# Attention with key tiles in twos: two score tiles, then P-V of the two before

## The chip, the cores and the metric

The kernel runs on one core of a Trainium2 chip. The time is the device time in microseconds (us) from launch to end. Five engines work beside one another, each through its own queue in order: TensorE (PE, matmul), VectorE (DVE), ScalarE (ACT), GpSimd (POOL) and SyncE (SP), which here issues nearly all transfers. TensorE writes its results to eight PSUM banks of 128 partitions by 512 fp32 numbers. VectorE and ScalarE read them there; GpSimd doesn't.

## The reference

Two layers of multi-query attention, each followed by a SwiGLU feed-forward, on 2048 tokens of width 448, all in fp32:

```
def A(x):  # 16 heads of 28, one shared key and value head
    q, k, v = x @ wq (per head), x @ wk, x @ wv
    p = softmax(q k^T * 28**-0.5)
    return (p v, heads side by side) @ wo
def B(x):  # width 1792
    return (silu(x @ w_gate) * (x @ w_up)) @ w_down
x = x + A(layernorm(x)); x = x + B(layernorm(x))
x = x + A(layernorm(x)); x = x + B(layernorm(x))
```

## The kernel before, in words

**Stages.** Projections of q, k and v, then the attention proper (`scores`), then the feed-forward, twice. The change is in `scores` alone. There is a second pass of the whole forward that runs only where row sums leave a bound (`full`); it isn't run here.

**Groups and steps.** Attention runs over 16 groups (`GR`: four chunks of 512 queries by four groups of four heads). In each group it goes over the 16 key tiles of 128 keys; one key tile is a step. A step issues, on TensorE, the transposed scores of four heads (lines 564 to 570): three waves of four matmuls, where the four heads sit on four strips of 32 rows of the array and the three waves are the parts of a product of split fp32 numbers. Three heads go to a tile of three banks (`three`, of which there are two, taken in turn) and the fourth to a single bank, bank 7 (`one`). ScalarE turns the single (line 573) and then the three (line 574) into exponentials in SBUF (`pt1`, `pt`). No maximum is subtracted there; it is folded into the scores by extra rows of q and k.

**P-V.** `pv` (line 604) multiplies the exponentials by the values (`vsb`, with a column of ones that gives the row sums). Its four heads sit on four strips of 32 columns of the array, and it is fp32, which shows as two matmul rows for each of the four. It runs two steps behind the scores and adds up in bank 6 over all 16 tiles of a group.

**End of a group.** `post` copies bank 6 to SBUF on VectorE (line 617) and gathers the four row sums with four transfers (line 620). `rest`, two steps later (`due`), waits for them, tests and inverts them on VectorE (lines 626 to 628), sends them to DRAM and back as a broadcast (630, 631), and on GpSimd normalises (638) and splits the result in high and low halves (lines 134, 135).

**What else is issued in a group.** The order of every queue is that of the program text. By key tile: `stack`, the q loads of the group after next, at tile 4 (line 380); `parts`, their split on GpSimd, at 7; `rows`, the transfer that puts the maxima into the split q and therefore waits for the split, at 9 (line 391); `load_wo` in groups 2 and 3 and `weights` (feed-forward weights, five transfers and a split on GpSimd) in groups 11 to 13, both at 8. In groups 5, 13 and 14 the steps of a layer norm come one per tile from tile 6: four statistics (`stat`, VectorE), `scale` (GpSimd: the reciprocal deviation `rstd`, lines 221 and 222) and, in 5 and 13, four `apply` (VectorE, line 229, which reads `rstd`). In groups 4, 8 and 12, at tile 10, `between_steps` puts the output projection of a chunk on TensorE, 48 matmuls into the free three and into bank 7, with four sums on VectorE; in 8 and 12 two flips (transposes) with it.

Of the kernel before, what the change touches and what calls it, by code (L numbers as in the profile page):

```python
# [8 lines left out]
F32 = mybir.dt.float32  # L9
F32R = mybir.dt.float32r  # L10
AF = mybir.ActivationFunctionType
ALU = mybir.AluOpType
# [3 lines left out]
P = 128  # L16
# [6 lines left out]
NT = S // P  # L23
# [3 lines left out]
FG = 2  # L27
SCALE = DH ** -0.5
# [26 lines left out]
def forward(  # L55
# [14 lines left out]
    nc = tc.nc  # L70
    fine, least, whole = fine or (None, None, None)
    KC = NC
# [14 lines left out]
    phase, banks, threes, live, turn = ExitStack(), [], [], set(), {}  # L87
# [33 lines left out]
    def halves(name):  # L121

        return pers.tile([P, 2, 512], F32R, tag="halves", name=name, bufs=2)
# [18 lines left out]
    vsb = pers.tile([P, NT, 32], F32, name="vsb")  # L142
# [158 lines left out]
    GR = [(c, g) for c in range(NC) for g in range(NG)]  # L301

    class Attention:
# [226 lines left out]
        def scores(self, ff):  # L530
            next(switch)
            with tc.tile_pool(name=f"at{self.layer}", bufs=1) as wp:
                woh = wp.tile([P, NG, D], F32R, name="woh")
                wol = wp.tile([P, NG, D], F32R, name="wol")
                on, accs, pts = {}, {}, {}
                todo, due = [], {}
# [21 lines left out]

                def step(n):

                    i, kt = divmod(n, NT)
                    three, one = threes[n % 2], banks[7]
                    q, k, ks = qts[i % 3], keys[kt // 4], slice(P * (kt % 4), P * (kt % 4) + P)
                    for z, (kp, part) in enumerate(((0, 0), (1, 0), (0, 1))):
                        for j in range(4):
                            js = slice(32 * j, 32 * j + 32)
                            nc.tensor.matmul(  # L567
                                three[:, j, :] if j < 3 else one, k[js, kp, ks], q[js, part, :],
                                start=(z == 0), stop=(z == 2), tile_position=(32 * j, 0),
                            )  # L570
                    pt = wp.tile([P, 3, 512], F32, name="pt", bufs=3)
                    pt1 = wp.tile([P, 512], F32, name="pt1", bufs=2 if full else 3)
                    nc.scalar.activation(pt1, one, AF.Exp, scale=SCALE)  # L573
                    nc.scalar.activation(pt, three, AF.Exp, scale=SCALE)  # L574
                    pts[n] = [*(pt[:, j, :] for j in range(3)), pt1]

                def between_steps(n):

                    i, kt = divmod(n, NT)
                    free, one = threes[(n + 1) % 2], banks[7]  # L580
                    if full:
                        self.lent = free[:, 0, :]
                        self.advance(KC)
                        if kt == 11 and i + 1 < len(GR):
                            self.places[i + 1](free[:, 1, :])
                    if not todo or kt != 10:
                        return
                    c = todo.pop()
                    ks = list({8: (0, 1), 12: (2, 3)}.get(i, ()))
                    adds = []  # L590
                    for t in (1, 2, 3):
                        adds.append(outproj(c, t, free[:, t - 1, :]))
                        if ks:
                            flip(got, X0, [ks.pop(0)], one)
                    for f in adds:
                        f()
                    outproj(c, 0, one)()

                def pv(n):
                    i, kt = divmod(n, NT)  # L600
                    if kt == 0:
                        accs[i] = banks[6]
                    for j in range(4):
                        nc.tensor.matmul(  # L604
                            accs[i][32 * j : 32 * j + 32, :], vsb[:, kt, :], pts[n][j],
                            start=(kt == 0), stop=(kt == NT - 1), skip_group_check=True,
                        )
                    del pts[n]
                    if kt == NT - 1:
                        due[n + 4] = post(i)  # L610

                def post(i):

                    c, g = GR[i]
                    out2 = halves("o2").bitcast(F32)
                    oraw, rb = out2[:, 0, :], out2[:, 1, :]
                    nc.vector.tensor_copy(oraw, accs.pop(i))
# [32 lines left out]
                last = NT * len(GR)  # L650
                for n in range(last):
                    i, kt = divmod(n, NT)
                    if kt == 4 and 2 < i + 2 < len(GR):
                        self.stack(i + 2)
                    if kt == 7 and 2 < i + 2 < len(GR):
                        self.parts(i + 2)
                    if kt == 9 and 2 < i + 2 < len(GR) and not full:
                        self.rows(i + 2)
                    if i in (2, 3) and kt == 8:
                        load_wo(i - 2)  # L660
                    if n == NT and ff.nxt:
                        ff.nxt.below(nc.sync)
                    if kt == 8 and 10 < i <= 11 + FG:
                        ff.W[i - 11] = weights(i - 11)
                    step(n)
                    if not full:
                        between_steps(n)
                    if n > 1:
                        pv(n - 2)
                    if full:  # L670
                        between_steps(n)
                    if n in due:
                        due.pop(n)()
                    if i in (5, 13, 14) and kt > 5:
                        for f in {5: fs, 13: fs1, 14: ff.second[0][:5]}[i][kt - 6 : kt - 5]:
                            f()
                for n in (last - 2, last - 1):
                    pv(n)
                self.lent = None
                next(switch)  # L680
                ff.X[0] = X0
# [223 lines left out]
    fs, got = norm_steps(0)  # L905
# [64 lines left out]
```

## Time and profile before

| | us |
|---|---|
| three runs: median (lowest to highest) | 2043.53 (2042.91 to 2044.38) |
| profiled execution, span from first to last instruction | 2041.5 |
| attention of the first layer, first to last exponential's start | 73.9 to 593.0 |
| attention of the second layer | 1082.9 to 1601.4 |
| busy: TensorE / ScalarE / VectorE / GpSimd | 2018.5 / 1311.0 / 460.0 / 536.7 |

The page gives the profiled execution by its span; the runs' median is 2.0 us above it. In a row of a group stand the line, the engine, the operation, output from input with their shapes, the count, the busy time in us, the mean in ns of one and the idle time ahead of it with what ended it. In a row of the timeline stand the start, the duration, the engine, the line and the operation; a bracket gives the idle time ahead of it. Rows of the same kind that lie close are merged (x4). In a row of a table of stretches stand the stretch, its length, the busy time and count of each engine (PE, weight loads, DVE, ACT, POOL), the granted clock of TensorE (0.99 to 1.00 in both attention stages), the share of the DMA engines and GB/s.

### The profile page before, as it was taken

The page shows a single profiled execution, that of the slowest core. Times are in us where ns is not written, and L with a number is a line of the kernel's source. Part 1 is how long each engine was busy: PE and PEld are TensorE (multiplying, and loading weights), DVE is VectorE, ACT ScalarE, POOL GpSimd, SP SyncE. Part 2 cuts the span into 40 slices and gives each one's busy share as a digit, 9 for nine tenths or more (in the row PEclk, how much of TensorE's full clock was granted, in tenths as well). Part 3 has the DMA queues.
Part 4 walks back from the last instruction along what each step waited for, and adds up shares of the span by engine and source line. Part 5 has one row for each costly group of instructions (what it writes and reads, how often), then busy time and mean ns, then how long its engine had stood idle before and what let it go on. Part 6 is the DMA issues. An engine that isn't in the chain of part 4 may idle for free.

```text
span 2041.5 us, 43675 instructions
## 1 busy us (share of the span) xinstructions
PE 2018.5 (99%) x18627; PEld 1275.7 (62%) x18627; DVE 460.0 (23%) x890; ACT 1311.0 (64%) x2152; POOL 536.7 (26%) x601
## 2 busy tenths in 40 slices
PE   8999999999999999999999999999999999999998
PEld 7533434334348999999883334343343689988887
DVE  6300101001104323222451001010011242232322
ACT  3699898997973333333348998979979533333332
POOL 4313121021302333333341221111222122333320
PEclk9999999999999999999999999999999999999999
DMA  4201000011100111100031110100110000111102
GB/s 146 66 22 28 21 12 22 12 37 27 32 12 19 31 31 31 31 16 26 21 93 34 30 30 12 22 12 22 27 45 13 25 17 20 31 31 31 31 1 74
DMA packets 76512, 63.44 MB, mean 31 GB/s; under 512 B 22904, under 2 KB 63224, under 8 KB 76312
## 3 DMA queue, kind: packets, MB, share of 16 engines
q1 hardware_dynamic: 74580, 58.93, 10.4%
q8 instruction: 147, 2.41, 0.5%
q10 hardware_dynamic: 1732, 1.66, 0.3%
q14 instruction: 53, 0.43, 0.1%
HBM read 47.72 MB, written 12.32 MB: 29 GB/s over the span
## 4 chain that ended last, share of the span: by engine, by line
PE 50%; ACT 46%; DVE 1%; issue 1%; DMA 1%; POOL 0%; ACTq 0%; SPq 0%; DVEq 0%; POOLq 0%
PE bank L292 39%; ACT pt L574 31%; ACT pt L573 15%; PE bank L272 4%; PE three L551 2%; PE bank L551 2%; PE bank L246 1%; PE bank L604 1%; DMA wr<-in_A_wk_dram 1%; PE three L567 0%; DVE xl L253 0%; DMA kt<-stage 0%; DVE xn L229 0%; PE bank L398 0%; DVE vt L505 0%
## 5 line engine op out<-in xcount | busy, mean ns | idle before, releaser
L574 ACT ACTIVATE pt<-three 128x1536 f32<-128x1536 f32 x512 | 741.2, 1448 | 0.0
L604 PE MATMUL bank<-pt,vsb 128*32 128x512 f32 x4096 | 547.0, 606 | 0.5 <-ACT pt L574 0.5
L567 PEld LDWEIGHTS three<-qstack,keys 32*128 32x128 f32 x4608 | 252.9, 183 | 449.7 <-ACT pt L573 393.2
L567 PE MATMUL three<-qstack,keys 32*128 32x512 f32 x4608 | 498.5, 426 | 2.3 <-DVE vt L505 1.1
L567 PE MATMUL bank<-qstack,keys 32*128 32x512 f32 x1536 | 493.5, 426 | 2.9 <-ACT pt L573 2.9
L292 PE MATMUL bank<-xh,wgh 64*128 64x512 f32 x1728 | 447.6, 390 | 0.4
L292 PE MATMUL bank<-xh,wgl 64*128 64x512 f32 x1404 | 368.2, 390 | 0.0
L573 ACT ACTIVATE pt<-bank 128x512 f32<-128x512 f32 x512 | 305.8, 597 | 74.3 <-PE bank L567 68.1
L292 PE MATMUL bank<-xl,wgh 64*128 64x512 f32 x1296 | 335.1, 390 | 0.0
L292 PE MATMUL bank<-wdh,h 64*128 64x448 f32 x1792 | 331.2, 364 | 1.2 <-ACT h L827 0.8
L292 PEld LDWEIGHTS bank<-xh,wgh 64*128 64x128 f32 x1728 | 262.9, 184 | 19.1 <-DVE xl L253 1.5
L743 POOL TENSOR_TENSOR xres<-stage,xres 128x448 f32<-128x448 f32 x108 | 127.4, 1199 | 497.9 <-ACT stage L742 497.9
L638 POOL TENSOR_TENSOR o<-o 128x512 f32<-128x512 f32 x32 | 41.1, 1285 | 821.5 <-DMA o<-rd 748.5
L292 PEld LDWEIGHTS bank<-wdh,h 64*128 64x128 f32 x1792 | 242.5, 184 | 15.2 <-issue 2.7
L567 PEld LDWEIGHTS bank<-qstack,keys 32*128 32x128 f32 x1536 | 244.3, 183 | 4.5 <-ACT pt L573 4.3
L299 ACT COPY seen<-bank 128x1 f32<-128x1 f32 x664 | 81.7, 163 | 247.3 <-PE bank L292 244.4
L292 PEld LDWEIGHTS bank<-xh,wgl 64*128 64x128 f32 x1404 | 216.6, 184 | 13.8
L292 PE MATMUL bank<-wdl,h 64*128 64x448 f32 x896 | 217.7, 366 | 0.0
L825 ACT ACTIVATE sg<-bank 128x512 f32<-128x512 f32 x112 | 67.3, 601 | 220.0 <-PE bank L292 214.9
L292 PEld LDWEIGHTS bank<-xl,wgh 64*128 64x128 f32 x1296 | 196.3, 184 | 10.5
L604 PEld LDWEIGHTS bank<-pt,vsb 128*32 128x32 f32 x4096 | 80.9, 108 | 190.0 <-issue 175.2
L826 DVE TENSOR_TENSOR sg<-bank,sg 128x512 f32<-128x512 f32 x112 | 77.4, 691 | 500.0 <-ACT sg L825 491.1
(115 smaller groups left out, 1736.6 us busy)
## 6 DMA issues: line engine op xcount, KB each, us to landing
o<-rd SPq DMA_DIRECT2D x32, 256.0 KB
qd<-stage SPq DMA_DIRECT2D x32, 224.0 KB
qraw<-qd SPq DMA_DIRECT2D x128, 56.0 KB
wdr<-in_B_w_down_dram SPq DMA_DIRECT2D x28, 224.0 KB
wr<-in_B_w_gate_dram SPq DMA_DIRECT2D x28, 192.0 KB
wr<-in_B_w_up_dram SPq DMA_DIRECT2D x28, 192.0 KB
out_dram<-xres SPq DMA_DIRECT2D x15, 224.0 KB
wrk<-kt SPq DMA_DIRECT2D x8, 256.0 KB
```

The costliest lines, as they stand in the source:

```text
L272: nc.tensor.matmul(po, a, b, start=(i == 0), stop=(i == len(seq) - 1))
L292: nc.tensor.matmul(po, a, b, start=start, stop=stop, skip_group_check=True)
L299: nc.scalar.copy(seen[:, i : i + 1], po[:, 0:1])
L551: nc.tensor.matmul(po[:, 0:D], a[:, g, ts_], b[:, g, :], start=(g + z == 0), stop=(g == NG - 1 and z == 2))
L567: nc.tensor.matmul(three[:, j, :] if j < 3 else one, k[js, kp, ks], q[js, part, :], start=(z == 0), stop=(z == 2), tile_position=(32 * j, 0),)
L573: nc.scalar.activation(pt1, one, AF.Exp, scale=SCALE)
L574: nc.scalar.activation(pt, three, AF.Exp, scale=SCALE)
L604: nc.tensor.matmul(accs[i][32 * j : 32 * j + 32, :], vsb[:, kt, :], pts[n][j], start=(kt == 0), stop=(kt == NT - 1), skip_group_check=True,)
L638: nc.gpsimd.tensor_tensor(rb, oraw, rb, ALU.mult)
L743: nc.gpsimd.tensor_tensor(r, s, r, ALU.add)
L825: nc.scalar.activation(sg, pg[0], AF.Silu)
L826: nc.vector.tensor_tensor(sg, pg[1], sg, ALU.mult)
```

## The change

The 16 key tiles of a group go in eight cycles of two. In cycle m the two banks 6 and 7 are single a and single b, and they change roles from cycle to cycle. A cycle issues:

1. TensorE: scores of the even tile into the first three and single a; ScalarE: exponential of a, then of the three.
2. TensorE: scores of the odd tile into the second three and single b; VectorE copies b to SBUF (`pt1`); ScalarE: exponential of the three, then of the copy, in place.
3. The norm steps of this cycle, if any (now two per cycle, from cycle 3).
4. TensorE: P-V of both tiles of the cycle before, into single a; VectorE copies the result to SBUF (first cycle of a group) or adds it to what is there.
5. `rest` of a finished group (in cycle 2 of the next one), and the output projection (cycle 5), which uses the first three and single b.

So the sum over a group's tiles is in PSUM over two tiles and in SBUF over the eight cycles; `post` has no copy of its own. `pt` and `pt1` have four buffers in place of three. `stack` stands at cycle 2, `parts` at 3, and at 4 `rows`, `load_wo` and `weights`, in this order.

```diff
-                def step(n):
+                def tile_scores(n, three, one):
...
-                    three, one = threes[n % 2], banks[7]
...
-                    pt = wp.tile([P, 3, 512], F32, name="pt", bufs=3)
-                    pt1 = wp.tile([P, 512], F32, name="pt1", bufs=2 if full else 3)
-                    nc.scalar.activation(pt1, one, AF.Exp, scale=SCALE)
-                    nc.scalar.activation(pt, three, AF.Exp, scale=SCALE)
+                    pt = wp.tile([P, 3, 512], F32, name="pt", bufs=4)
+                    pt1 = wp.tile([P, 512], F32, name="pt1", bufs=4)
                     pts[n] = [*(pt[:, j, :] for j in range(3)), pt1]
+                    return pt, pt1
+
+                def singles(m):
+                    return banks[6 + m % 2], banks[7 - m % 2]
+
+                def cycle(m):
+                    a, b = singles(m)
+                    pt, pt1 = tile_scores(2 * m, threes[0], a)
+                    nc.scalar.activation(pt1, a, AF.Exp, scale=SCALE)
+                    nc.scalar.activation(pt, threes[0], AF.Exp, scale=SCALE)
+                    pt, pt1 = tile_scores(2 * m + 1, threes[1], b)
+                    nc.vector.tensor_copy(pt1, b)
+                    nc.scalar.activation(pt, threes[1], AF.Exp, scale=SCALE)
+                    nc.scalar.activation(pt1, pt1, AF.Exp, scale=SCALE)
...
-                def pv(n):
-                    i, kt = divmod(n, NT)
-                    if kt == 0:
-                        accs[i] = banks[6]
-                    for j in range(4):
-                        nc.tensor.matmul(
-                            accs[i][32 * j : 32 * j + 32, :], vsb[:, kt, :], pts[n][j],
-                            start=(kt == 0), stop=(kt == NT - 1), skip_group_check=True,
-                        )
-                    del pts[n]
-                    if kt == NT - 1:
-                        due[n + 4] = post(i)
+                def pv(m, to):
+                    i, u = divmod(m, NT // 2)
+                    for y in range(2):
+                        n = 2 * m + y
+                        for j in range(4):
+                            nc.tensor.matmul(
+                                to[32 * j : 32 * j + 32, :], vsb[:, n % NT, :], pts[n][j],
+                                start=(y == 0), stop=(y == 1), skip_group_check=True,
+                            )
+                        del pts[n]
+                    if u == 0:
+                        accs[i] = halves("o2").bitcast(F32)
+                        nc.vector.tensor_copy(accs[i][:, 0, :], to)
+                    else:
+                        nc.vector.tensor_tensor(accs[i][:, 0, :], to, accs[i][:, 0, :], ALU.add)
+                    if u == NT // 2 - 1:
+                        due[m + 3] = post(i)
...
+                ops = {}
+                for i, todo_ in ((5, fs), (13, fs1), (14, ff.second[0][:5])):
+                    for n, f in enumerate(todo_):
+                        ops.setdefault((i, 3 + n // 2), []).append(f)
...
+                    cycle(m)
+                    for f in ops.get((i, u), ()):
+                        f()
+                    if m:
+                        pv(m - 1, singles(m)[0])
+                    if m in due:
+                        due.pop(m)()
+                    between_cycles(m)
+                pv(last - 1, banks[6])
```

More of the change, by code (lines that the diff above doesn't have):

```diff
@@ L649, in scores @@
                 ff.second = norm_steps(2)
[L650 to L653, printed above, removed]
+                ops = {}
+                for i, todo_ in ((5, fs), (13, fs1), (14, ff.second[0][:5])):
+                    for n, f in enumerate(todo_):
+                        ops.setdefault((i, 3 + n // 2), []).append(f)
+                last = NT // 2 * len(GR)
+                for m in range(last):
+                    i, u = divmod(m, NT // 2)
+                    if u == 2 and 2 < i + 2 < len(GR):
                         self.stack(i + 2)
-                    if kt == 7 and 2 < i + 2 < len(GR):
+                    if u == 3 and 2 < i + 2 < len(GR):
                         self.parts(i + 2)
-                    if kt == 9 and 2 < i + 2 < len(GR) and not full:
+                    if u == 4 and 2 < i + 2 < len(GR) and not full:
                         self.rows(i + 2)
-                    if i in (2, 3) and kt == 8:
+                    if i in (2, 3) and u == 4:
                         load_wo(i - 2)
-                    if n == NT and ff.nxt:
+                    if m == NT // 2 and ff.nxt:
                         ff.nxt.below(nc.sync)
-                    if kt == 8 and 10 < i <= 11 + FG:
+                    if u == 4 and 10 < i <= 11 + FG:
                         ff.W[i - 11] = weights(i - 11)
[L665 to L678, printed above, removed]
+                    cycle(m)
[7 more added lines that the diff above has]
+                pv(last - 1, banks[6])
                 self.lent = None
```

21 lines of the change are left out of this document (10 added, 11 removed).

## The prediction

> **What bounds the kernel now.** First the page: totals and the costly groups.
>
> ```profile
> span 2041.5 us, 43675 instructions
> ...
> PE 2018.5 (99%) x18627; PEld 1275.7 (62%) x18627; DVE 460.0 (23%) x890; ACT 1311.0 (64%) x2152; POOL 536.7 (26%) x601
> ...
> L573 ACT ACTIVATE pt<-bank 128x512 f32<-128x512 f32 x512 | 305.8, 597 | 74.3 <-PE bank L567 68.1
> ```
>
> TensorE is busy almost throughout, so the question is what paces the attention stages. I looked at their length and at ScalarE's waits in them.
>
> ```profile
> 73.90:593.00 519.10, 517.61 (x5245) 196.84 (x5249) 49.10 (x144) 484.34 (x511) 105.04 (x106) 0.99 0.09 22
> ```
>
> ```profile
> ACT pt L573 <- PE bank L567: 68.1, 10, 11.3
> ```
>
> The first layer's 256 steps run 519 us from the first exponential to the last. The second layer has the same stage, so I put half of the 68.1 us of long waits into each; 255 intervals in 519.1 - 34.1 = 485.0 us are 1.90 us per key tile, 3.80 per pair. The waits are the out-projections (11.3 us the longest). In between, ScalarE shows no idle time and looks like the bound. The timeline behind one out-projection says otherwise.
>
> ```profile
> 494.46 0.60 ACT L573 ACTIVATE pt<-bank 128x512 f32<-128x512 f32 x1 [11.33 <-PE bank L567]
> 494.95 1.45 ACT L574 ACTIVATE pt<-three 128x1536 f32<-128x1536 f32 x1
> 496.28 0.60 ACT L573 ACTIVATE pt<-bank 128x512 f32<-128x512 f32 x1
> ...
> 498.09 0.63 ACT L573 ACTIVATE pt<-bank 128x512 f32<-128x512 f32 x1
> ...
> 501.89 0.60 ACT L573 ACTIVATE pt<-bank 128x512 f32<-128x512 f32 x1
> ...
> 503.77 0.60 ACT L573 ACTIVATE pt<-bank 128x512 f32<-128x512 f32 x1
> ```
>
> ```profile
> 493.08 0.50 PE L567 MATMUL three<-qstack,keys 32*128 32x512 f32 x3
> ...
> 493.42 0.40 PE L567 MATMUL three<-qstack,keys 32*128 32x512 f32 x3
> ...
> 493.65 0.40 PE L567 MATMUL three<-qstack,keys 32*128 32x512 f32 x3
> ...
> 493.99 1.06 PE L604 MATMUL bank<-pt,vsb 128*32 128x512 f32 x8
> 494.98 0.51 PE L567 MATMUL three<-qstack,keys 32*128 32x512 f32 x3
> 495.11 0.49 PE L567 MATMUL bank<-qstack,keys 32*128 32x512 f32 x1
> ...
> 501.37 0.39 PE L567 MATMUL bank<-qstack,keys 32*128 32x512 f32 x1
> ```
>
> Where scores stood ready, ScalarE made two steps in 498.09 - 494.46 = 3.63 us, 1.815 each. Later it needs 503.77 - 501.89 = 1.88. TensorE, by contrast, goes from scores to scores in 494.98 - 493.08 = 1.90 although ScalarE stood idle before: it isn't waiting, it is that slow. One step has 0.91 for scores (493.08 to 493.99) and 0.99 for P-V. So TensorE paces the steps, and ScalarE has 0.08 us of hidden slack per step: its rows overlap (0.60 long, but the next starts 0.49 later), so the slack is no gap on the page.
>
> Why 0.91: the second and third waves of four matmuls are 0.23 apart, but the last wave holds the array 0.34 (493.65 to 493.99) before P-V starts. Each change between scores and P-V costs about 0.1.
>
> **The change part by part: the pace.** Two score tiles in a row, then two P-V tiles in a row, so two changes per pair go. The end of the layer has two P-V together already:
>
> ```profile
> 592.79 1.92 PE L604 MATMUL bank<-pt,vsb 128*32 128x512 f32 x16
> 594.99 1.06 PE L604 MATMUL bank<-pt,vsb 128*32 128x512 f32 x8 [0.27 <-ACT pt L574]
> ```
>
> Sixteen matmuls span 1.92 where eight span 1.06, and the next work starts 0.07 before a span's end (493.99 + 1.06 against 494.98), so a P-V pair holds TensorE 1.85 against 1.98. A score pair is 0.34 + 4 x 0.23 + 0.34 = 1.60 against 1.82. TensorE alone could do a pair in 3.45. That isn't the new pace, since three other chains close each cycle. Time 0 is the start of the first single's exponential:
> - ScalarE: 2 x 1.815 = 3.63, and one of the four now reads SBUF. The nearest rows are a 512-wide cast from SBUF and the single's exponential from PSUM: 621 - 597 = 24 ns, so 3.65.
> - Single a: exponential 0.60, release 0.05 (494.46 + 0.60 to the single's matmul at 495.11), P-V pair 1.85, scores to their third wave 0.57, wave to exponential 0.52 (501.37 to 501.89): 3.59.
> - VectorE: P-V pair ends at its span's 1.92, VectorE starts 0.14 later (594.99 + 1.06 to 596.19), sum 0.69, release 0.05, rest of the scores and drain 0.8: 3.60.
>
> ```profile
> L827 ACT CAST h<-sg 128x512 fp32r<-128x512 f32 x112 | 69.6, 621 | 99.3 <-DVE sg L826 87.2 <-POOL onl L135 12.1
> ```
>
> ```profile
> L617 DVE COPY o<-bank 128x512 f32<-128x512 f32 x32 | 22.1, 692 | 659.1 <-PE bank L604 659.1
> ```
>
> ```profile
> 596.19 0.69 DVE L617 COPY o<-bank 128x512 f32<-128x512 f32 x1 [22.47 <-PE bank L604]
> ```
>
> All three lie within 0.1 of each other, so I take the largest, 3.65 (bounds: 3.59, if ScalarE overlaps better than it has shown, and 3.80, if VectorE's 512 new operations arrive late). Gain (3.80 - 3.65) x 256 pairs = 38.4 us; bounds 54 and 0. The copies and sums themselves, 512 x 0.69 = 353 us, are covered: 1.4 per pair of 3.65, while VectorE was busy 49 of 519 us. But that cover holds only while VectorE is punctual, and its queue is in order.
>
> [...]
>
> **What now stands in VectorE's queue.** The norms of the next stage are issued between a cycle's copy and its sum: statistics in groups 5, 13 and 14, and in groups 5 and 13, at cycle 5, `scale` on GpSimd and at once `apply(0)` on VectorE, which waits for GpSimd's rstd. Before, that wait cost nothing, since VectorE had one copy per group. Group 13, which starts at 503.77:
>
> ```profile
> 511.81 0.17 DVE L626 TENSOR_SCALAR under<-rs 128x16 f32<-128x16 f32 x1 [4.42 <-DMA rs<-o]
> ...
> 512.53 0.25 DVE L628 RECIPROCAL rs<-rs 128x16 f32<-128x16 f32 x1
> ...
> 532.33 1.78 DVE L229 TENSOR_SCALAR xn<-xres,mv,rstd 128x448 f32<-128x448 f32 x4 [16.68 <-POOL rstd L222]
> ```
>
> ```profile
> 520.29 1.28 POOL L638 TENSOR_TENSOR o<-o 128x512 f32<-128x512 f32 x1 [30.44 <-DMA o<-rd]
> ...
> 524.32 1.28 POOL L135 TENSOR_TENSOR qstack<-qraw,qstack 128x512 fp32r<-128x512 f32 x1
> 525.63 1.05 POOL L134 TENSOR_SCALAR wgh<-wr 128x1024 fp32r<-128x1024 f32 x1
> ...
> 531.29 1.01 POOL L222 TENSOR_TENSOR rstd<-rstd,halfn 128x4 f32<-128x4 f32 x1
> ```
>
> ```profile
> 514.23 0.58 SPq L631 DMA_DIRECT2D o<-rd  x1
> ...
> 516.67 0.40 SPq L130 DMA_DIRECT2D wr<-in_B_w_gate_dram  x1
> ...
> 525.62 0.57 SPq L391 DMA_DIRECT2D qstack<-rows  x1
> ```
>
> VectorE sat 16.68 us there, because rstd stands behind the group's normalisation, the q split and the whole weight split. Now behind that wait stand the sum that frees single a, with it the odd tile's scores, then every exponential. Its end in the changed kernel, from the group's first exponential: the last sum of the group before ends at 0.65 + 1.92 + 0.14 + 0.69 = 3.4; the reciprocal block comes behind cycle 2's sum, 2 x 3.65 + 3.4 = 10.7, and takes 0.97 (511.81 to 512.78): 11.7. The DMA of the reciprocals and its landing 1.45 (512.78 to 514.23): 13.1. The broadcast back lands after 5.4 to 6.1; group 13 had 6.06 with q and weight loads right behind it, which now go before and long after it; group 5 had 5.4 without weight loads (its rows are below), and I take that: 18.5. Normalising and q split 5.31 (520.29 to 525.60): 23.8. Then the queue of SP: the row load (`rows`), which waits for the q split, now stands ahead of the weight loads, where it stood behind them, so these start only at 24.4. How long they take, from group 11:
>
> ```profile
> 445.28 0.41 SPq L130 DMA_DIRECT2D wr<-in_B_w_gate_dram  x1
> ...
> 447.49 1.12 SPq L158 DMA_DIRECT2D wdr<-in_B_w_down_dram  x1
> ```
>
> ```profile
> 449.50:451.30 1.80, 1.80 (x24) 0.66 (x20) 0.00 (x0) 1.80 (x3) 1.72 (x3) 1.00 0.39 131
> 451.30:452.00 0.70, 0.70 (x12) 0.37 (x12) 0.00 (x0) 0.70 (x2) 0.70 (x1) 1.00 0.12 39
> ```
>
> The DMA engines fall from 0.39 to 0.12 at 451.3, 6.0 after the first issue: landed at 30.5. Weight split and rstd 6.67 (525.63 to 532.30): rstd at 37.2, against 28.5 before.
>
> VectorE reaches the wait at 5 x 3.65 + 1.4 = 19.7. ScalarE still has cycle 5 and the even tile of cycle 6, then nothing. After rstd: `apply` 0.45 (1.78 for four), sum 0.69, release 0.05, scores and drain 0.9, P-V 1.85, scores and exponential 1.07: the next even exponential starts at 42.2 instead of 7 x 3.65 = 25.6. Loss 16.7 us, in each layer.
>
> Group 5 has no weights:
>
> ```profile
> 261.58 1.78 DVE L229 TENSOR_SCALAR xn<-xres,mv,rstd 128x448 f32<-128x448 f32 x4 [10.73 <-POOL rstd L222]
> ```
>
> ```profile
> 254.87 1.29 POOL L638 TENSOR_TENSOR o<-o 128x512 f32<-128x512 f32 x1 [36.26 <-DMA o<-rd]
> ```
>
> ```profile
> 249.47 0.58 SPq L631 DMA_DIRECT2D o<-rd  x1
> ```
>
> Rstd reaches VectorE 6.71 after the normalising starts: 18.5 + 6.7 = 25.2, and by the same sum a loss of 4.7 per layer. Together 2 x (16.7 + 4.7) = 42.8 us. Bounds: if the loads came in 3.3 (issue alone, 445.28 to 448.61) 37; if in 9 (516.67, where group 13 issued, to 525.63), 49. The statistics share VectorE with the sums in 12 cycles; they wait for nothing and cost me nothing, at the upper end 1 us.
>
> **Out-projection.** It moves behind the P-V of its cycle and keeps its 48 matmuls. P-V, 0.99, no longer stands between it and the next scores, but a P-V pair, 1.85, went ahead of it on ScalarE's cover, and VectorE's last sum on the single (near the 0.69 above), once under P-V, is exposed: between -1 and +1.5 for each of six; I take +0.4 from between, 2.5 us. Its last input is ready before 18.5 + 4.0 = 22.5 (520.29 to 524.32, when the q split is under way) and is asked for by the twelfth matmul of a row that starts at 5 x 3.65 + 0.65 + 1.85 = 20.8: close, and taken as no wait. The reciprocals' own wait (4.42 us in group 13, for the DMA) goes, since one more cycle lies between; nothing waited behind it. The output weights of groups 2 and 3 and the first weights of groups 11 and 12 also come later behind the row load; they are used a group later or more, so nothing waits.
>
> **Sum.** -38.4 + 42.8 + 2.5 = +7 us on the profiled span of 2041.5; the runs' median of 2043.53 is 2.0 above the span, so about 2051.
>
> **Rivals.** 1. Faster, by one mechanism: rstd comes early, so that VectorE's wait is short. Both stalls would have to total under 36 us for a tie, rstd in group 13 before about 33.7; if they vanished wholly, 2051 - 43 = 2008, with only group 13's gone 2018. For it: the wait costs nothing until about 20. Against: GpSimd's and SP's order as written, and 28.5 even before the row load moved ahead. 18%.
> 2. The pace doesn't fall: sums reach single a late and odd scores wait, because all three chains are within 0.1 us. At 3.80 the stalls are all that is left: 2051 + 38 = 2089; at 3.72, 2069. For it: each cycle has two more hand-overs between engines. Against: each is 0.05 to 0.14 in the rows. 17%.
> 3. Something else in VectorE's queue adds a wait (the out-projection's inputs late, reciprocals late): 2055 to 2075. 15%, a few of them with compensating errors near no change.
>
> **How the numbers follow.** My forecast, pace 3.62 to 3.70 and stalls as worked, 2042 to 2064, has 50%. A difference under 0.2%, 4 us, can't be told from no change. Forecast: 0.38 slower, 0.12 same; rival 1 faster 0.18; rival 2 slower 0.17; rest 0.09 slower, 0.04 same, 0.02 faster. Faster 0.20, same 0.16, slower 0.64. For eight in ten the range runs from part of rival 1, 2034, into rival 2, 2080.
>
> **What would show it.** Pace: even exponentials 3.65 us apart in quiet groups; 3.59 or 3.80 tell which chain closes. Switching: scores to scores at 0.23. Stalls: a wait of VectorE's `xn` for rstd of 17 us in group 13 and 5 in group 5, and behind it idle ScalarE of 16 and 4 us before an exponential, four times in all. Weight loads issued behind the row load. The prediction is wrong if ScalarE has no such gaps (then faster), or if the gaps are there and the pace is above 3.70 (then well slower).

## The result and the profile after

The changed kernel takes 2071.97 us (median of four runs, 2067.13 to 2075.12) against 2043.59 for the kernel before (2042.91 to 2044.38). The ratio is 1.0135, with a 95% interval of 1.0123 to 1.0147: slower, by 28.4 us. The profiled execution of the changed kernel has a span of 2070.7 us, 29.2 more than that of before.

The page of the changed kernel: the span and the busy time of the engines (share of the span, number of instructions).

```profile
span 2070.7 us, 44582 instructions
...
PE 2003.9 (97%) x18627; PEld 1348.2 (65%) x18627; DVE 788.3 (38%) x1370; ACT 1286.5 (62%) x2152; POOL 536.5 (26%) x601
```

TensorE's busy time fell by 14.6 us (2018.5 before) while the span grew by 29.2, so TensorE now stands idle for 66.8 us where it did for 23. ScalarE's busy time fell by 24.5.

**The quiet groups.** In groups 9, 10 and 11 of the first layer no norm step and no output projection is issued. The timeline of the kernel before, at the single's exponential with which group 9 and then group 12 begin, 48 key tiles apart:

```profile
370.96 0.60 ACT L573 ACTIVATE pt<-bank 128x512 f32<-128x512 f32 x1
...
462.16 0.60 ACT L573 ACTIVATE pt<-bank 128x512 f32<-128x512 f32 x1
```

The timeline of the changed kernel at the same two places (first and last row), and between them one cycle of the cross-engine chain:

```profile
369.20 0.64 ACT L583 ACTIVATE pt<-bank 128x512 f32<-128x512 f32 x1
...
369.89 1.92 PE L618 MATMUL bank<-pt,vsb 128*32 128x512 f32 x16
...
371.94 0.69 DVE L627 TENSOR_TENSOR o<-bank,o 128x512 f32<-128x512 f32 x1 [1.25 <-PE bank L618]
...
372.69 0.50 PE L566 MATMUL bank<-qstack,keys 32*128 32x512 f32 x1
...
372.86 0.67 ACT L583 ACTIVATE pt<-bank 128x512 f32<-128x512 f32 x1
...
373.58 0.64 PE L618 MATMUL bank<-pt,vsb 128*32 128x512 f32 x4
...
457.70 0.65 ACT L583 ACTIVATE pt<-bank 128x512 f32<-128x512 f32 x1
```

Before, a pair takes (462.16 - 370.96) / 24 = 3.800 us; after, (457.70 - 369.20) / 24 = 3.688. Over 256 pairs that is a gain of 28.7 us. In the cycle shown, P-V starts at 369.89 and again at 373.58, 3.69 apart: VectorE's sum starts 2.05 after the first P-V and takes 0.69, the odd tile's single follows 0.06 later, and from there it is 0.89 to the next P-V. There is no slack on that way.

**The stalls.** The chain of waits of the changed kernel through group 13 of the first layer (start, duration, what):

```profile
512.03 5.15 DMA o<-rd
...
521.43 1.27 POOL qstack L135
522.72 0.56 SPq L391
523.32 0.47 SPq L130
...
524.94 5.61 DMA wr<-in_B_w_up_dram
...
531.86 2.34 POOL wgl L135
...
536.31 1.02 POOL rstd L222
...
537.78 0.70 DVE o L627
```

Everything that the sum waits for stands here in order: the broadcast of the reciprocals, GpSimd's q split, the row load (L391), only then the weight loads (L130), the weight split, rstd, and behind it `apply` and the sum (L627). Rows of the timeline of the same group, VectorE's wait and ScalarE's:

```profile
498.85 0.64 ACT L583 ACTIVATE pt<-bank 128x512 f32<-128x512 f32 x1
...
521.22 0.60 ACT L583 ACTIVATE pt<-bank 128x512 f32<-128x512 f32 x1
...
537.36 0.51 DVE L229 TENSOR_SCALAR xn<-xres,mv,rstd 128x448 f32<-128x448 f32 x1 [18.28 <-POOL rstd L222]
...
539.86 1.45 ACT L587 ACTIVATE pt<-three 128x1536 f32<-128x1536 f32 x1 [16.71 <-PE three L566]
...
540.10 3.64 PE L618 MATMUL bank<-pt,vsb 128*32 128x512 f32 x16
...
545.09 0.60 ACT L583 ACTIVATE pt<-bank 128x512 f32<-128x512 f32 x1 [3.26 <-PE bank L566]
...
545.75 1.92 PE L618 MATMUL bank<-pt,vsb 128*32 128x512 f32 x16
```

The group begins at 498.85 and rstd reaches VectorE at 537.36, 38.5 us in. The even exponentials at 521.22 and 545.09 are 23.87 apart in place of 3.69. And there is a second thing: the P-V pair behind the wait takes 3.64 where the next takes 1.92. The table of stretches (the last three numbers of a row are the granted clock, the share of the DMA engines and GB/s), first group 5, then group 13:

```profile
250.00:260.00 10.00, 6.17 (x71) 2.92 (x64) 3.19 (x7) 7.23 (x8) 6.50 (x8) 0.89 0.02 6
260.00:264.00 4.00, 4.00 (x25) 0.76 (x17) 1.54 (x3) 1.97 (x2) 0.66 (x2) 0.50 0.00 0
...
523.50:537.40 13.90, 0.00 (x0) 0.00 (x0) 0.04 (x1) 0.00 (x0) 6.26 (x6) 0.52 0.20 55
537.40:541.00 3.60, 2.48 (x17) 1.08 (x21) 1.86 (x4) 1.14 (x1) 0.24 (x1) 0.50 0.01 2
541.00:544.50 3.50, 3.50 (x24) 1.09 (x20) 1.38 (x3) 0.83 (x2) 0.66 (x2) 0.51 0.00 0
544.50:548.00 3.50, 3.43 (x44) 1.42 (x44) 1.38 (x4) 2.91 (x3) 0.24 (x1) 1.00 0.00 0
```

While TensorE stands idle its granted clock falls to half (0.52 on the mean from 523.5 to 537.4), and it is still at 0.50 when work is there again. In group 13 TensorE has no work from 521.3 until the sum ends (537.78 + 0.70 in the chain, 538.5), which is 17.2 us; the clock is back at 1.00 only in the stretch from 544.5, 6 us after the restart.

| pair interval with VectorE's wait | rstd reaches VectorE, into the group | from there to the next even exponential | interval | lost (less 3.69) |
|---|---|---|---|---|
| first layer, group 5 | 25.1 | 7.45 | 10.24 | 6.55 |
| first layer, group 13 | 38.5 | 7.73 | 23.88 | 20.19 |
| second layer, group 5 | 25.1 | 7.35 | 10.14 | 6.45 |
| second layer, group 13 | 37.9 | 7.49 | 22.97 | 19.28 |

The losses sum to 52.5 us. Two smaller ones come with them, read from the intervals between even exponentials in the timeline: the six output projections lose 3.6 us more than before (first layer: 10.9, 11.6 and 11.7 against 10.2, 11.1 and 11.4; second layer: 10.9, 12.1 and 11.7 against 10.2, 11.1 and 11.2), and the twelve cycles with two statistics take 3.81, 0.12 over the others, 1.5 in all. Together -28.7 + 52.5 + 3.6 + 1.5 = +28.9, against +29.2 between the spans.

### The profile page after: what moved, and what is told of

Same layout as the page of the kernel before. It is cut to its first block, busy times and chain, and to the rows that moved or that the text cites. A ratio compares the mean times of both kernels' runs of the same rounds, so it can differ in the third digit from the quotient of the medians.

```text
span 2070.7 us, 44582 instructions
## 1 busy us (share of the span) xinstructions
PE 2003.9 (97%) x18627; PEld 1348.2 (65%) x18627; DVE 788.3 (38%) x1370; ACT 1286.5 (62%) x2152; POOL 536.5 (26%) x601
## 4 chain that ended last, share of the span: by engine, by line
PE 90%; issue 3%; DVE 2%; DMA 2%; POOL 2%; ACT 1%; SPq 0%; ACTq 0%; POOLq 0%; DVEq 0%
PE bank L292 38%; PE bank L618 22%; PE three L566 15%; PE bank L566 6%; PE bank L272 4%; PE three L551 2%; PE bank L551 2%; PE bank L246 1%; DMA wr<-in_A_wk_dram 1%; DMA wr<-in_B_w_up_dram 1%; DMA o<-rd 0%; DVE xn L229 0%; DVE xl L253 0%; POOL o L656 0%; POOL rstd L222 0%
## 5 line engine op out<-in xcount | busy, mean ns | idle before, releaser
L566 PE MATMUL bank<-qstack,keys 32*128 32x512 f32 x1536 | 487.8, 428 | 44.9 <-DVE o L627 41.4
L618 PE MATMUL bank<-pt,vsb 128*32 128x512 f32 x4096 | 502.3, 608 | 0.4
L566 PE MATMUL three<-qstack,keys 32*128 32x512 f32 x4608 | 454.3, 423 | 4.6 <-ACT pt L584 3.1
L566 PEld LDWEIGHTS three<-qstack,keys 32*128 32x128 f32 x4608 | 260.6, 184 | 285.3 <-ACT pt L584 184.2
L587 ACT ACTIVATE pt<-three 128x1536 f32<-128x1536 f32 x256 | 382.5, 1494 | 39.5 <-PE three L566 39.5
L584 ACT ACTIVATE pt<-three 128x1536 f32<-128x1536 f32 x256 | 379.5, 1483 | 0.0
L618 PEld LDWEIGHTS bank<-pt,vsb 128*32 128x32 f32 x4096 | 108.2, 110 | 255.1 <-issue 159.9
L586 DVE COPY pt<-bank 128x512 f32<-128x512 f32 x256 | 177.1, 692 | 251.5 <-PE bank L566 250.2
L627 DVE TENSOR_TENSOR o<-bank,o 128x512 f32<-128x512 f32 x224 | 154.7, 690 | 264.1 <-PE bank L618 252.2
L583 ACT ACTIVATE pt<-bank 128x512 f32<-128x512 f32 x256 | 162.2, 634 | 89.6 <-PE bank L566 86.1
```

The lines of the kernel that those rows point to most:

```text
L566: nc.tensor.matmul(three[:, j, :] if j < 3 else one, k[js, kp, ks], q[js, part, :], start=(z == 0), stop=(z == 2), tile_position=(32 * j, 0),)
L583: nc.scalar.activation(pt1, a, AF.Exp, scale=SCALE)
L584: nc.scalar.activation(pt, threes[0], AF.Exp, scale=SCALE)
L586: nc.vector.tensor_copy(pt1, b)
L587: nc.scalar.activation(pt, threes[1], AF.Exp, scale=SCALE)
L618: nc.tensor.matmul(to[32 * j : 32 * j + 32, :], vsb[:, n % NT, :], pts[n][j], start=(y == 0), stop=(y == 1), skip_group_check=True,)
```

## The experiments

All ratios are to the kernel before, run on the same chip. Runs without an interval are single ones, with a profile.

### Take the wait out of VectorE's queue (apply_later)

The four `apply` of groups 5 and 13 are issued one group later, when rstd has long been made; `scale` stays where it was.

```diff
-                for i, todo_ in ((5, fs), (13, fs1), (14, ff.second[0][:5])):
+                for i, todo_ in ((5, fs[:5]), (6, fs[5:]), (13, fs1[:5]), (14, ff.second[0][:5] + fs1[5:])):
```

> The four apply operations of groups 5 and 13 are issued one group later (cycles of groups 6 and 14), where rstd has long been made; nothing else moves. Theory (VectorE's wait for rstd holds the sum behind it, and so the scores and ScalarE): both gaps vanish, 2 x (20.2 + 6.6) less 0 = about -52 us against the changed kernel, about 2019 us, faster than before by 24; ScalarE shows no gap over 1 us outside the out-projections and the start. Rival (the gaps come from GpSimd's or SP's lateness itself, for instance the q of the group after next): the gaps stay near 16 and 4 us and the time near 2070.

Measured: 2020.51 us (2017.43 to 2021.31), ratio 0.9882 (0.9866 to 0.9899): 51.5 less than the changed kernel, for 52.5 lost in the four intervals. The table of stretches where the changed kernel stood idle, and in the timeline two even exponentials, two cycles apart, behind the output projection of group 12, with three rows between them:

```profile
512.00:530.00 18.00, 18.00 (x198) 7.86 (x200) 6.92 (x10) 17.98 (x20) 9.80 (x11) 1.00 0.16 45
```

```profile
489.01 0.61 ACT L583 ACTIVATE pt<-bank 128x512 f32<-128x512 f32 x1
...
492.15 0.67 ACT L588 ACTIVATE pt<-pt 128x512 f32<-128x512 f32 x1
492.67 0.64 ACT L583 ACTIVATE pt<-bank 128x512 f32<-128x512 f32 x1
493.15 1.50 ACT L584 ACTIVATE pt<-three 128x1536 f32<-128x1536 f32 x1
...
496.33 0.67 ACT L583 ACTIVATE pt<-bank 128x512 f32<-128x512 f32 x1
```

TensorE is busy for all 18 us, at full clock. The order of one queue turns the change from a loss of 28 us into a gain of 23 over the kernel before. The second answer is used below: where scores stand ready, ScalarE alone does a pair in (496.33 - 489.01) / 2 = 3.66.

### The weight loads ahead of the row load again (rows_behind)

```diff
-                    if u == 4 and 2 < i + 2 < len(GR) and not full:
-                        self.rows(i + 2)
                     if i in (2, 3) and u == 4:
...
+                    if u == 4 and 2 < i + 2 < len(GR) and not full:
+                        self.rows(i + 2)
                     cycle(m)
```

> Only the row load goes back behind the weight loads in SP's queue. Theory (the weight loads wait behind it for the q split, and rstd waits for the weights): the weight split of group 13 starts right behind the q split, 23.9 instead of 31 to 32 us into the group; rstd 7.7 us earlier, so about -15 us, 2057. Group 5 keeps its gap of 6.6. Rival (the loads are no part of it, GpSimd's work alone makes rstd late): no change, 2072.

Measured: 2055.74 us (2053.84 to 2058.1), ratio 1.0055 (1.0038 to 1.0072). The timeline:

```profile
514.09 0.59 SPq L649 DMA_DIRECT2D o<-rd  x1
...
514.72 0.48 SPq L130 DMA_DIRECT2D wr<-in_B_w_gate_dram  x1
...
525.75 0.58 SPq L391 DMA_DIRECT2D qstack<-rows  x1
```

```profile
532.32 0.51 DVE L229 TENSOR_SCALAR xn<-xres,mv,rstd 128x448 f32<-128x448 f32 x1 [11.22 <-POOL rstd L222]
```

The loads go out 0.6 behind the broadcast in place of 11.3, VectorE's wait falls from 18.28 to 11.22, and the intervals of group 13 from 23.88 and 22.97 to 17.16 and 15.99. The place of the row load in SP's queue is worth 13.7 us by these intervals and 16.2 by the medians. The rest stays, because rstd still stands behind the normalisation and the weight split.

### Keep TensorE busy while it waits (warm)

Thirty transposes of the identity in group 5 and 140 in group 13, which nobody reads, fill most of the wait.

```diff
                     nc.scalar.activation(pt, threes[0], AF.Exp, scale=SCALE)
+                    for _ in range({(5, 6): 30, (13, 6): 140}.get(divmod(m, NT // 2), 0)):
+                        nc.tensor.transpose(threes[1][:, 0, 0:P], ident, ident)
                     pt, pt1 = tile_scores(2 * m + 1, threes[1], b)
```

> The waits stay. In cycle 6 of groups 5 and 13 TensorE gets 30 and 140 transposes of the identity into the second three ahead of the odd tile's scores, 3.3 and 15.3 us of work in time that it would wait; the scores overwrite them. Theory (after the wait TensorE runs at half the granted clock, 0.50 in the rows, and that makes the loss 2.5 to 2.7 us longer each time): granted clock stays at 1.00, the P-V pair after the wait takes 1.85 instead of 3.57, each loss shrinks by 2.5 to 2.7, together about -10 us, 2062. Rival (the longer loss is only the chain's restart at the normal clock): no change, or slower by what the transposes hold up.

Measured: 2065.48 us (2062.61 to 2065.94), ratio 1.0107 (1.009 to 1.0123); the profiled span is 2060.9. The table of stretches behind the wait, and the timeline:

```profile
534.70:540.00 5.30, 4.44 (x48) 2.00 (x52) 3.34 (x6) 2.17 (x3) 0.97 (x4) 1.00 0.02 5
```

```profile
519.17 15.50 PE L586 MATMUL three<-ident 128*128 128x128 f32 x140
...
534.81 0.51 DVE L229 TENSOR_SCALAR xn<-xres,mv,rstd 128x448 f32<-128x448 f32 x1 [17.59 <-POOL rstd L222]
...
536.87 1.92 PE L620 MATMUL bank<-pt,vsb 128*32 128x512 f32 x16
...
539.80 0.60 ACT L583 ACTIVATE pt<-bank 128x512 f32<-128x512 f32 x1 [1.00 <-PE bank L566]
```

The clock stays at 1.00, the P-V behind the wait takes 1.92, and from rstd to the next even exponential it is 539.80 - 534.81 = 4.99, in all four places (4.98 to 4.99) against 7.35 to 7.73: the halved clock costs 30.02 - 19.96 = 10.1 us. The median of the runs fell by 6.5 for the 10 that were forecast; the span fell by 9.8, and the profiled execution is the fastest of the four. The intervals of group 13 were 20.45 and 22.22, because rstd itself came 37.8 and 39.6 us into the group: the weight loads land sooner or later from layer to layer and run to run (from the first issue to the split 7.4 and 6.8 us in the changed kernel's two layers, 6.7 in the first layer here), which I did not look into.

### What closes the quiet cycle (short_sums, half_b, half_b_short_sums)

Two chains in the changed kernel come to 3.68 or 3.69: VectorE's (the P-V, the sum, the odd tile's scores), and single a's (its exponential, the P-V, the even tile's scores). Three kernels shorten the one, the other, or both. The first takes the changed kernel and sums 128 of the 512 columns:

```diff
-                        nc.vector.tensor_tensor(accs[i][:, 0, :], to, accs[i][:, 0, :], ALU.add)
+                        nc.vector.tensor_tensor(accs[i][:, 0, 0:128], to[:, 0:128], accs[i][:, 0, 0:128], ALU.add)
```

> VectorE's sums cover 128 of the 512 columns; the other columns of the attention output keep the first cycle's value only, so part of the sums is left out. A sum takes about 0.3 us instead of 0.69. Theory (the quiet pace of 3.684 per pair is closed by P-V, VectorE's sum, the odd scores): the odd single's first matmul no longer stands 0.14 behind the others and the pace falls to ScalarE's own 3.66. Rival (single a's exponential and the P-V behind it close the pace): it stays at 3.68. Both leave the gaps of groups 5 and 13.

Measured: 2065.34 us. The timeline at the start of groups 9 and 12:

```profile
366.11 0.64 ACT L583 ACTIVATE pt<-bank 128x512 f32<-128x512 f32 x1
...
454.51 0.69 ACT L583 ACTIVATE pt<-bank 128x512 f32<-128x512 f32 x1
```

The pace is (454.51 - 366.11) / 24 = 3.683, all but unchanged. VectorE alone does not close the cycle. The single intervals say more: from 362 us, behind the output projection of group 8, they are 3.66, ScalarE's own, as long as single a's exponential grows from 0.61 to 0.67 us; later in the group it is 0.70 long, and they are 3.68 to 3.69, the length of single a's chain: 0.70 and then 0.05, 1.85 and 1.09 to its next exponential. The 6.6 us less in time come mostly from the statistics, whose cycles are at 3.66 to 3.69 here, and from the four intervals with the wait, which lose 48.5 us in place of 52.5.

The second takes `apply_later` and relieves ScalarE, which ends single a's exponential sooner:

```diff
-                    nc.vector.tensor_copy(pt1, b)
+                    nc.vector.tensor_scalar(pt1, b, 0.001, None, ALU.max)
                     nc.scalar.activation(pt, threes[1], AF.Exp, scale=SCALE)
-                    nc.scalar.activation(pt1, pt1, AF.Exp, scale=SCALE)
+                    nc.scalar.activation(pt1[:, 0:256], pt1[:, 0:256], AF.Exp, scale=SCALE)
```

> From apply_later, which has no long waits for rstd (2020.5, pace 3.684). ScalarE makes the exponential of the copied odd single over 256 of its 512 columns only; the others keep what the copy put there (scores raised to at least 0.001, so that row sums stay positive). So a part of the computation is left out, and ScalarE's own work falls from 3.66 to about 3.45 per pair; VectorE's and TensorE's stay. Three theories of what paces the quiet groups. ScalarE: 3.45 to 3.50, 1965 to 1975. Single a's chain: its exponential now ends 0.60 after it starts instead of 0.70, so 0.60 + 0.05 + 1.85 + 0.58 + 0.51 = 3.59, 256 x 0.094 = 24 less, 1996. VectorE's chain: P-V start to sum 2.05, sum 0.69, release 0.06, scores to the third wave 0.57, drain 0.32 = 3.69, and no change: 2020. I take VectorE's, since in the changed kernel both chains come to 3.68 to 3.69 and only one of them gets shorter here.

Measured: 2019.72 us, with

```profile
362.63 0.60 ACT L583 ACTIVATE pt<-bank 128x512 f32<-128x512 f32 x1
...
451.16 0.60 ACT L583 ACTIVATE pt<-bank 128x512 f32<-128x512 f32 x1
```

that is 3.689. The pace does not move, so what holds it here is not ScalarE. But the edit takes less from ScalarE than the 0.2 us that were expected of it: behind the output projection of group 12, where scores stand ready, a pair takes 488.56 - 484.98 = 3.58 for 3.66. The row is 0.24 shorter (0.43 for 0.67), yet the next one starts only 0.09 sooner. The third does both:

> As half_b, and the sums take 128 of 512 columns (as in short_sums), so that VectorE's chain loses about 0.3 too (its sum 0.39 or less instead of 0.69). If single a's chain and VectorE's chain close the cycle side by side, which is what I now hold, it is the two together that move it: 3.59, 1996, while short_sums alone and half_b alone leave 3.68. If ScalarE alone sets the pace, it is the same as half_b, 1965 to 1975. If something else closes it, 2020.

Measured: 1999.05 us, with

```profile
358.52 0.60 ACT L583 ACTIVATE pt<-bank 128x512 f32<-128x512 f32 x1
...
445.05 0.60 ACT L583 ACTIVATE pt<-bank 128x512 f32<-128x512 f32 x1
```

that is 3.605 on average; the median interval is 3.588. Neither of the two edits alone moves the pace, and both together do. So two limits lie side by side, and VectorE's chain is one of them. Which the other is, these kernels can't tell apart: 3.588 is the length worked out for single a's chain with an exponential of 0.60, but ScalarE's own 3.58 would give the same, since `half_b` shortens both. For single a's chain speak the intervals of `short_sums`, 3.68 to 3.69 where ScalarE alone does 3.66; no edit here shortens that chain and leaves ScalarE's work as it is.

### No copy (no_copy)

ScalarE makes the odd single's exponential straight from its bank, and VectorE's copy goes.

```diff
-                    nc.vector.tensor_copy(pt1, b)
+                    nc.scalar.activation(pt1, b, AF.Exp, scale=SCALE)
                     nc.scalar.activation(pt, threes[1], AF.Exp, scale=SCALE)
-                    nc.scalar.activation(pt1, pt1, AF.Exp, scale=SCALE)
```

The text on record has one thing the wrong way round: the odd single's exponential stands ahead of the second three's, where the copy stood, and not behind it.

> VectorE's copy of the odd single goes; ScalarE makes the exponential of single b straight from the bank, behind its second three, as it is done for single a. Theory: the copy pays by freeing bank b early. Without it the odd single's bank and the following even scores wait for ScalarE's last row of the cycle, and the pace is 3.83 per pair (the P-V of the next cycle, 0.05 after that row, then 1.85, scores and exponentials of the even tile, 7.65 over two cycles) against 3.684, so 256 x 0.15 = 38 us more: about 2108. The rival, that the exponential out of SBUF is what costs (0.52 behind it where the bank's row has 0.49) and VectorE's hand-over holds the cycle: pace 3.65, 2063. The four waits for rstd stay in either case.

Measured: 2103.78 us. The timeline:

```profile
379.32 0.60 ACT L583 ACTIVATE pt<-bank 128x512 f32<-128x512 f32 x1 [0.23 <-PE bank L566]
...
471.30 0.60 ACT L583 ACTIVATE pt<-bank 128x512 f32<-128x512 f32 x1 [0.16 <-PE bank L566]
```

The pace is (471.30 - 379.32) / 24 = 3.833, the length that was worked out. But the text speaks of the other order of the rows, in which bank b is what waits, so the number alone does not show that its path is the right one. ScalarE now shows waits for the scores. In the same stretch the odd tile's scores wait for the second three, which ScalarE now leaves a row later:

```profile
383.15 0.50 PE L566 MATMUL three<-qstack,keys 32*128 32x512 f32 x3 [0.24 <-ACT pt L587]
```

So the copy earns its time on VectorE: without it, in this order of ScalarE's rows, two P-V tiles in a row would be slower than the kernel before (3.80) even with no wait for rstd. The other order, the three first, was not run.

### Is TensorE the pace of the kernel before (before_two_waves)

```diff
-                    for z, (kp, part) in enumerate(((0, 0), (1, 0), (0, 1))):
+                    for z, (kp, part) in enumerate(((0, 0), (0, 1))):
...
-                                start=(z == 0), stop=(z == 2), tile_position=(32 * j, 0),
+                                start=(z == 0), stop=(z == 1), tile_position=(32 * j, 0),
```

> The kernel before, with one of the three score waves of each key tile left out (the high half of q by the low half of k, so the scores lack that part of their precision); everything else is as it was. Theory of the prediction: TensorE paces the kernel before at 1.896 per key tile, and ScalarE alone could do 1.815 to 1.83. With 0.23 us of TensorE's work less in each of 512 steps, ScalarE becomes the pace: 1.83, 512 x 0.066 = 34 us less, about 2010. The rival, that ScalarE already sets the pace before (no idle time shows ahead of its rows): 1.89 to 1.90, and about 2042.

Measured: 2009.72 us. The timeline, again 48 key tiles apart:

```profile
361.69 0.71 ACT L573 ACTIVATE pt<-bank 128x512 f32<-128x512 f32 x1
...
449.45 0.95 ACT L573 ACTIVATE pt<-bank 128x512 f32<-128x512 f32 x1
```

(449.45 - 361.69) / 48 = 1.828 per key tile against 1.900. With TensorE's work cut by 0.23, the step falls by 0.07 only, so TensorE had been the pace and another limit lies close below it. The mean hides two stretches. In the first nine steps shown the interval is 1.807, ScalarE's own, while the single's rows, 0.60 before, grow from 0.71 by 0.03 per step: that is what these rows look like while ScalarE is full. From 377.96 on they stay at 0.95 and the interval is 1.833, the length of the single's own loop: its exponential 0.95, 0.05 to the next scores into bank 7, 0.34 to their second wave, 0.49 to the next exponential.

### Both orders together (both)

`apply_later` and `rows_behind` in one kernel.

> The last four norm steps of groups 5 and 13 are issued in groups 6 and 14 (as in apply_later), and the row load also stands behind the weight loads (as in rows_behind). My theory: with the norm's apply out of VectorE's way nobody waits for rstd in a hurry, so the earlier weight loads are worth nothing: 2020.5, as apply_later, between 2017 and 2024, and intervals of group 13 at 3.69. The rival, that the row load ahead of the weights also costs something apart from VectorE's wait (a late split of the feed-forward's weights, a late q of the next group): 2015 or less.

Measured: 2019.75 us (2017.82 to 2020.6), ratio 0.9883 (0.9866 to 0.9899), the same as `apply_later` alone. Early weight loads are worth 14 to 16 us while VectorE waits for them, and nothing once it doesn't.

## Why the prediction was right, and where it was wrong

The direction, slower, was right, and 2072 lies in the range. The mechanism was the one predicted, at both ends: a shorter pace, and more than its gain lost in four waits of VectorE. But the sum said +7 and it came out at +29: outside the 2042 to 2064 that the forecast gave for itself.

- **TensorE paces the kernel before, at 3.80 per pair.** Right: 3.800 in the quiet groups, and `before_two_waves` shows what lies beneath, 1.807 for ScalarE alone, where 1.815 was read from two steps of which the first did not find it full.
- **Pace after 3.65, the largest of three chains; gain 38.4 us.** This term was mis-sized: 3.688, and 28.7 us. ScalarE's own was right (3.66 in `apply_later`). VectorE's chain, forecast at 3.60, is 3.69. The step that failed is "rest of the scores and drain 0.8": it is 0.89 (372.69 to 373.58). I had measured the hand-overs and estimated this one, and the prediction's own sum for the stall has the same way at 0.9. Single a's, forecast at 3.59, is the same length: its exponential was put at 0.60, and takes 0.64 to 0.70 where ScalarE's rows overlap, since ScalarE has hardly any slack. `half_b_short_sums` has 3.588 with an exponential of 0.60, but ScalarE's own pair is as short there, so it does not confirm the 3.59. That three chains lay within 0.1 us of each other was a warning in itself: the cycle takes the longest of them, so whichever was put too low decides.
- **What ScalarE pays for reading SBUF.** The rows gave ScalarE's own pace as 3.65, with 24 ns in it for the read from SBUF. Measured is 3.66, but both parts of the sum were off. Where ScalarE is full, the next row starts 0.520 us after one that reads SBUF and 0.477 after a single that reads PSUM (`apply_later`, from 492.15, 492.67 and 493.15): 43 ns, where the 24 had come from the lengths of two different operations. What was too long was the base, 3.63 for 2 x 1.807 = 3.61. ScalarE isn't what paces the kernel, so the difference decided nothing.
- **VectorE waits for rstd: 16.7 us in group 13 and 4.7 in group 5.** The place, the cause and the order of the queues were right: rstd 38.5 and 37.9 us into group 13 for a forecast of 37.2, 25.1 into group 5 for 25.2, the row load ahead of the weight loads, ScalarE idle 16.71 for a forecast of 16. `apply_later` gives back 51.5 us, so the stalls are the whole of the loss. Their size was 52.5 for a forecast of 42.8. Of the difference, 10.1 is the halved clock: the forecast had 5.0 from rstd to the next even exponential, `warm` measured 4.99, the changed kernel 7.35 to 7.73. I took the durations behind the wait from rows at full clock, without asking what a wait of 4 or 17 us does to it. Weight loads that landed later (7.4 us from the first issue, 523.32, to the split at 530.73, for 6.0) add 1.3 and 0.7 to rstd in group 13. The last even exponential ahead of each wait starts 0.4 to 0.5 us later than forecast, 22.4 us into the group for 6 x 3.65 = 21.9, which takes some 1.8 back.
- **Out-projection +2.5.** 3.6. **Statistics at nothing, 1 us at most.** 1.5: their 0.12 per cycle comes through, since VectorE's chain has no slack to hide it; with that chain shorter, in `short_sums`, it does not.
- **Rivals.** The first, an early rstd, gave 2008 with both stalls gone: `apply_later` is that case, at 2020.5; 9.7 of the 12.5 us between are the pace, and most of the rest the output projections and the statistics. The second, the pace not falling, had its direction: 3.688 lies a quarter of the way from 3.65 to 3.80, and its 2069 for a pace of 3.72 is near the result only because the clock's 10 us came on top. The third had the right interval and no mechanism.

What stays open: why the weight loads land at different times, which moves rstd in group 13 between 37.8 and 39.6 us in kernels whose queues are the same up to there, and may be why the changed kernel's runs spread over 8 us; and whether single a's chain or ScalarE's work is the second limit of the quiet cycle.

## What to carry to other kernels

When an engine that had a free queue is put on the path of every cycle, go through its queue for waits that used to cost nothing: moving one group of instructions to where their input is ready was worth 51.5 us, more than twice what the rest of the change gains (2020.5 against 2043.6). Where several chains of hand-overs close a cycle within a few per cent of each other, measure every link, and take the price of shortening one of them to be nothing until the others are shorter too. And price the work behind a long wait of TensorE too: in all four waits here, 3.8 to 17.2 us long, the granted clock fell to 0.50, and the P-V pair behind took 3.60 to 3.64 us in place of 1.92.

## What the runs showed of the hardware

**The clock.** The granted clock is 0.99 to 1.00 on the mean in both attention stages of the kernel before, and the prediction looked no further. The mean hides a stretch at 0.50 in the first steps (75.1 to 81.9 us), and ahead of the stage the same trace has what the forecast lacked. TensorE's timeline:

```profile
15.12 4.30 PE L246 MATMUL bank<-ident,xn 128*128 128x128 f32 x16 [5.34 <-DVE xn L229]
...
29.80 1.91 PE L246 MATMUL bank<-ident,xn 128*128 128x128 f32 x16
```

After 5.34 us without work sixteen transposes take 4.30 us, most of them 0.21 apart, where sixteen like them take 1.91 later, 0.11 apart; from 14 to 20 us the granted clock is 0.50. In the changed kernel TensorE's idle time is 17.2 and 16.5 us in groups 13 and 3.8 us in groups 5, and in all four the clock falls to half, 2.0 to 4.8 us into it. In `rows_behind` it is 0.55 on the mean from 526 to 531 us, within a wait of 10.14 us. The P-V pair behind each of the changed kernel's four waits takes 3.60 to 3.64 in place of 1.92, and the clock is at full only 5.0 to 5.9 us after the restart; each wait costs 2.4 to 2.7 us on top of itself (7.35 to 7.73 from rstd to the next even exponential, against 4.99 in `warm`). With transposes whose results nobody reads in the wait, the clock is 1.00 throughout (`warm`, group 13 of the first layer, 519.7 to 545 us).

The stretches at half clock in the changed kernel's four waits are 6.83, 20.48, 6.83 and 17.07 us long: two, six, two and five times the shortest of that trace, 3.41 us (76.8 to 80.2, behind a wait of 1.73 us). How long a wait has to be for the clock to fall was not shown. Had I looked at the rows above for what a long wait does, the forecast would have been 10 us closer.

**ScalarE's rows.** Here a row's length said whether the engine was full, and the idle time ahead of it did not: the single's exponential takes 0.60 in the kernel before, where ScalarE has slack, and grows from 0.71 to 0.95 in `before_two_waves` while it is full, with no gap shown in either. Nor was the length what a row cost: halving one took 0.24 us off the row and 0.09 off the time to the next start (`half_b`).
